# Retention, then a Mish feed-forward, on one core: block 0's second product by sub-block products, block 5's first product likewise, and output stores regrouped

## The chip, the cores and the metric

The kernel runs on one core of one Trainium2 chip. The metric is the time of one execution on the device in microseconds (us). Engines are called TensorE (PE, with PEld for its weight loads), VectorE (DVE), ScalarE (ACT), GpSimd (POOL) and SyncE (SP), which issues nearly all DMAs.

## The reference

`q`, `k`, `v` are 4 x 8 x 768 x 64 (batch, head, position, feature). A linear recurrence with a decay per head gives y, and y (3072 tokens by 512) goes through a feed-forward of width 2048:

```
for t in range(S):
    state = gamma * state + outer(k[t], v[t])
    y[t] = scale * (q[t] @ state)
x = y.transpose(0, 2, 1, 3).reshape(3072, 512)
h = x @ w_in                       # 512 x 2048
g = h * tanh(softplus(h))          # Mish
out = g @ w_out                    # 2048 x 512, float32
```

## The kernel before

**Tiling.** The sequence is cut into 24 chunks of 128 positions, and the chunks into eleven blocks: block 0 has four chunks (512 tokens), blocks 1 to 10 have two (256 tokens). For each chunk, q and k are scaled to fp16 and transposed; scores k·q are masked; "outer" products of k and v update the state; "present" (masked scores times v) and "past" (state times q) make y, which is copied to `xt` as the input of the feed-forward.

**Weights.** w_in and w_out come as four slices of 512 rows or columns each (`FPS` = 4 groups of 128), loaded in fp32 (`load_w`) and cast to fp16 (`cast_win`, `cast_wout`).

**First product** (`g1`): h = w_in · xt, in PSUM banks of 128x512, each followed by a Mish on ScalarE. Block 0 takes 16 banks (u = 0 to 15) with matmuls of 512 columns; blocks 1 to 5 take 8 with matmuls of 256 columns. Blocks 6 to 10 (`blk >= MIX`, `mixed_in`) compute two of the four w_in slices by seven sub-products instead of eight (a Strassen-like scheme): sums of weight quarters (`in_sums`, made once in blocks 4 and 5, kept in `wsum`), sums of xt quarters (`x_sums`, per block), 56 matmuls of 128 columns for these slices and 32 of 256 columns for the two other slices; partial results are kept in `hsum` tiles.

**Second product.** Block 0 computes g · w_out plainly: 16 groups by 4 token tiles, 64 matmuls of 512 columns into four banks (L649), with the attention work of block 1 placed between them by a table `plan`. Blocks 1 to 10 (`seven`) use seven sub-products over the whole width, with sums of w_out quarters (`weight_sums`, tiles `tmat`, t1 to t4) and sums of g (`sums_a`, `sums_b`, `sums_c`, tiles `gsum`, s1 to s4); ScalarE takes snapshots (`snap`), VectorE adds and writes the output tile `osb`.

**Order.** The schedule is written by hand: each engine runs its instructions in the order of the source, and waits on semaphores. `turn_two` transposes q and k of chunks 4 and 5 on TensorE into one PSUM tile `t_ps` and copies them out in four pieces; from chunk 6 on, GpSimd casts (`casts_qk`, `casts_v`) and SP transposes by DMA (`turn_by_dma`). `cast_behind` casts the coming chunks inside `seven`, behind a small copy (`summed`) that makes GpSimd wait until VectorE has made certain sums; `second_of` does the same for blocks 6 and later. Stores are queued in a list with a due slice, and `store_due` issues them from the loop over u of the following block; so SP issues, in one order, loads, DMA transposes and stores, each of which waits for what it needs with all later ones behind it. `get_ready(blk + 1)` makes outer products and scores of the next block, in slice u = 5 of blocks 1 to 3's first product; blocks 3 and later prepare the block after the next in `retain`.

Of the kernel before, what the change touches and what calls it, by code (L numbers as in the profile page):

```python
# [16 lines left out]
def kernel(  # L17
# [9 lines left out]
    nc = tc.nc  # L27
# [172 lines left out]
    def cast_win(s, by_tile=False):  # L200
        src = wtmps.pop(("in", s))
        wins[s] = []
        for j in range(2):
# [6 lines left out]
                nc.vector.tensor_copy(t, src[:, :, at0:at0 + TB // 2])  # L210
            wins[s].append(t)

    def cast_wout(s, on_act=False):
        src = wtmps.pop(("out", s))
        t = cpool.tile([P, FPS, d_model], FP16, name=f"wout{s}")
        if on_act:
            for f in range(0, FPS, 2):
                nc.scalar.copy(t[:, f:f + 2], src[:, f:f + 2])
        else:
            nc.vector.tensor_copy(t, src)  # L220
        wouts[s] = t

    def store_due(now):
        while stores and stores[0][0] <= now:
# [403 lines left out]
    def g1(blk, u):  # L628
        nt = BLOCKS[blk] * C
        per = TB // nt  # L630
        h_ps = g1_bank(blk, u)
        for j in range(per):
            s, f = divmod(u * per + j, FPS)
            for bp in range(NBP):
                nc.tensor.matmul(  # L635
                    h_ps[:, j], wins[s][f // 2][:, bp, f % 2 * P:(f % 2 + 1) * P], xts[blk][:, bp, :nt],
                    start=(bp == 0), stop=(bp == NBP - 1))
# [9 lines left out]
    def g2_mm(o_ps, blk, t, fb, cols=slice(None)):  # L647
        s, f = divmod(fb, FPS)
        nc.tensor.matmul(  # L649
            o_ps, gts[blk, fb][:, t * P:(t + 1) * P], wouts[s][:, f, cols],  # L650
            start=(fb == 0), stop=(fb == NFB - 1))
# [7 lines left out]
    def g2_out(o_ps, t, due):  # L659
        osb = op.tile(list(o_ps.shape), FP32, name="osb", tag="osb")  # L660
        if t == 0:
            nc.scalar.copy(osb, o_ps)
        else:
            nc.vector.tensor_copy(osb, o_ps)
        stores.append((due, out_rows(0, t), osb))

    def weight_sums(half):
        n, hf = NFB // 2, d_model // 2
        if half == 0:
            tmats.extend(  # L670
                wstage.tile([P, 2, n, hf], FP16, name="tmat", tag="wt", bufs=4)
                for _ in range(2))
            gsums.extend(
                wstage.tile([P, 4, n, P], FP16, name="gsum", tag="wt", bufs=4)
                for _ in range(2))
        f = slice(half * FPS, (half + 1) * FPS)
        t1, t2 = tmats[0][:, 0, f], tmats[0][:, 1, f]
        t3, t4 = tmats[1][:, 0, f], tmats[1][:, 1, f]
        b11, b12 = wouts[half][:, :, :hf], wouts[half][:, :, hf:]
        b21, b22 = wouts[half + 2][:, :, :hf], wouts[half + 2][:, :, hf:]  # L680
        sub = ALU.subtract
        return [
            lambda: nc.vector.tensor_tensor(t1, b12, b11, op=sub),
            lambda: nc.vector.tensor_tensor(t2, b22, t1, op=sub),
            lambda: nc.vector.tensor_tensor(t3, b22, b12, op=sub),
            lambda: nc.vector.tensor_tensor(t4, b21, t2, op=sub),
        ]
# [20 lines left out]
        nc.vector.tensor_tensor(s4, a12, s2, op=ALU.subtract)  # L708

    def in_sums(j):  # L710
        t = cpool.tile([P, 4, 2, TB // 2], FP16, name=f"wsum_{j}")
        wsums.append(t)
# [104 lines left out]
    def seven(blk, masks, hooks, last):  # L817
        n, hf = NFB // 2, d_model // 2
        px = pxps.tile([P, hf], FP32, name="o_ps", tag="px")
        pb = mmps.tile([P, hf], FP32, name="o_ps", tag="mm")  # L820
        osb = [op.tile([P, d_model], FP32, name="osb", tag="osb") for _ in range(2)]

        def a(i, j):
            return lambda f: gts[blk, j * n + f][:, i * P:(i + 1) * P]
# [136 lines left out]
    def first_block():  # L961
# [74 lines left out]
        def cast_qk():  # L1036
            for a in range(2):
                cast_pair(2, "q", a, qs_two)
            for a in range(2):
                cast_pair(2, "k", a)  # L1040
            for a in range(2):
                cast_pair(2, "v", a, vs_two)

        def turn_two():
# [5 lines left out]
            for a in range(2):  # L1050
                i = slice(a * (HP // 2), (a + 1) * (HP // 2))
                for j, nm in enumerate("qk"):
                    taken(pairs[2, nm + "t"][:, i], t_ps[:, j, i], False)

        def sum_weights(half, n):
            if not weight_left:
# [1 line left out]
            for _ in range(n):  # L1058
                weight_left.pop(0)()

        plan = {
            9: [(cast_wout, 0)],
            12: [(cast_wout, 1)],
            16: [(cast_wout, 2), (load_more,), (cast_qk,)],
            17: [(sum_weights, 0, 3)],
            23: [(cast_wout, 3, True)],
            25: [(turn_two,)],
            26: [(pair_scores, 2, 0)],
            27: [(pair_scores, 2, 1)],
            28: [(sum_weights, 0, 1), (turn_both, CPB + 2)],  # L1070
            29: [(outer_two,)],
            30: [(present_two,), (sum_weights, 1, 1)],
            31: [(y_two,)],
        }
        o_tiles = [None] * CPB
        for u in range(2 * NFB):
            if u < 2:
                if u == 0:
                    open_in(2)
            elif u < NFB:  # L1080
                g1(0, u)
            elif u < 2 * NFB - 2:
                w = u - NFB
                if w == 0:
                    for t in range(CPB):
                        pool, tag = (pxps, "px") if t == 0 else (mmps, "mm")
                        o_tiles[t] = pool.tile([P, d_model], FP32, name="o_ps", tag=tag)
                for t in range(CPB):
                    if t == CPB - 1 and w == 1:
                        g2_mm(o_tiles[t], 0, t, 0)  # L1090
                    if t < CPB - 1 or w > 0:
                        g2_mm(o_tiles[t], 0, t, w)
            else:
                for t in range(CPB // 2) if u % 2 == 0 else range(CPB // 2, CPB):
                    for w in range(NFB - 2, NFB):
                        g2_mm(o_tiles[t], 0, t, w)
                    g2_out(o_tiles[t], t, 0)
            for fn, *args in plan.get(u + 1, ()):
                fn(*args)

    def u_banks():
        t = atps.tile([P, 2, TB], FP32, name="u_ps", tag="at")
# [50 lines left out]
    def next_one(g):  # L1153
        load_to(g + 3)
# [21 lines left out]
    def cast_behind(blk, i):  # L1176
        g = first[blk] + (6 if blk == 1 else 8)
        if ncast[0] < min(g, NCK):
            nc.gpsimd.tensor_copy(summed, gsums[blk % 2][:, i, NFB // 2 - 1, P - 1:])  # L1179
            if blk == 1:  # L1180
# [2 lines left out]
                for n in range(g - 2, g):  # L1183
                    casts_v(n)
                ncast[0] = g
            elif blk + 1 >= MIX:
                cast_to(g - 2)
                casts_qk(g - 2)
                ncast[0] = g
            else:  # L1190
                cast_to(min(g, nload[0]))

    def tight(blk):

# [1 line left out]

    def plan_of(blk):
        a = first[blk] + 4
        plan = {u: [] for u in (0, 1, 5)}
        if tight(blk):  # L1200
            plan[5] = [(get_ready, blk + 1)]
# [10 lines left out]
    for blk in range(1, len(BLOCKS)):  # L1212
        last = blk + 1 == len(BLOCKS)
        plan = plan_of(blk)
        if blk >= MIX:
# [14 lines left out]
        if not last:  # L1230
            later = blk + 2 if ONE <= blk < len(BLOCKS) - 2 else None
            hooks = [[(retain, blk + 1, later)],
                     [(next_one, first[blk] + 6)] if blk + 1 >= MIX else
                     [(next_two, first[blk] + 6, tight(blk))] if blk >= ONE else
                     [(turn_load, first[blk] + 4)] if blk == 1 else
                     [(next_chunk, first[blk] + 5), (turn_load, first[blk] + 6)],
                     [(finish, blk + 1)] if later is None else []]
# [34 lines left out]
```

## Time and profile before

| What | Value |
|---|---|
| Time, median of 3 runs | 196.81 us (196.01 to 197.21) |
| The profiled execution: its own time, its span | 196.27 us, 194.5 us |
| Granted TensorE clock | 0.998 |
| TensorE's share of the chain that ended last | 93% |
| Block 0, first product / second product with what lies between | 19.5 to 31.6 / 31.6 to 48.9 us |
| Blocks 1, 2, 3 begin at | 48.86, 63.68, 78.52 us |
| Blocks 4, 5, 6, 7 begin at | 93.75, 108.20, 122.64, 136.85 us |
| Last store issued | 192.0 us |

The profile is one execution, seen from the span's start. Busy time is what the records of an engine cover; TensorE's matmuls are pipelined, so one matmul's own duration (273 ns for 256 columns) is longer than the distance to the next (109 ns), and sums are made with distances. "Idle before" names what an engine waited for before an instruction. The chain that ended last is followed back from the end; where TensorE is in it without a gap, a shorter engine elsewhere wins nothing. A block begins with the first matmul of its first product.

### The profile page before, as it was taken

The numbers are of one execution on the slowest core, as the hardware profiler recorded it, in microseconds if no ns is written. First come the engines' busy times: TensorE is split into PE (matmuls) and PEld (weight loads), VectorE is DVE, ScalarE is ACT, GpSimd is POOL, SyncE is SP. The second block draws the span as 40 slices with busy tenths as digits, with TensorE's granted clock in tenths as the row PEclk, the third lists the DMA queues.
The fourth block names the chain that finished last, engine by engine and source line by source line (L and its number), as shares of the span: only waits on it lengthen the run. The fifth ranks groups of instructions, "written<-read, shape, count | busy, mean of one in ns | idle before, by whom it ended". The sixth has DMA issues, their size and how long they took to land.

```text
span 194.5 us, 6886 instructions
## 1 busy us (share of the span) xinstructions
PE 189.6 (97%) x2996; PEld 154.0 (79%) x2996; DVE 128.7 (66%) x248; ACT 99.5 (51%) x183; POOL 73.3 (38%) x96
## 2 busy tenths in 40 slices
PE   7998999999999999999999999999999999999994
PEld 7756444454888888888888888998998998988983
DVE  0796535889767378467884864965885885876462
ACT  3375764243553552554364364584574663763750
POOL 5262000549508746562826605525625700000000
PEclk9999999999999999999999999999999999999999
DMA  5999999999999999999999999889996250300202
GB/s 172 304 309 349 368 386 366 293 302 202 202 260 248 157 233 225 214 175 216 261 207 227 278 192 287 103 225 245 77 223 123 50 150 5 111 0 20 95 27 81
DMA packets 84285, 38.75 MB, mean 199 GB/s; under 512 B 57760, under 2 KB 78880, under 8 KB 84256
## 3 DMA queue, kind: packets, MB, share of 16 engines
q1 hardware_dynamic: 84112, 38.28, 84.7%
q8 instruction: 23, 0.38, 0.9%
q10 hardware_dynamic: 144, 0.05, 0.1%
q14 instruction: 6, 0.05, 0.1%
HBM read 27.31 MB, written 6.29 MB: 173 GB/s over the span
## 4 chain that ended last, share of the span: by engine, by line
PE 93%; DMA 3%; ACT 1%; DVE 1%; issue 1%; SPq 0%
PE o_ps L838 32%; PE h_ps L635 24%; PE h_ps L765 9%; PE h_ps L745 8%; PE o_ps L649 7%; PE y_ps L551 3%; DMA qfirst<-in_q_dram 3%; PE u_ps L479 1%; PE at L472 1%; PE t_ps L247 1%; PE y_ps L373 1%; PE h_ps L620 1%; PE at L443 1%; PE at L327 1%; DVE qk L259 1%
## 5 line engine op out<-in xcount | busy, mean ns | idle before, releaser
L635 PE MATMUL h_ps<-xt,win 128*128 128x256 f16 (+1 forms) x376 | 48.5, 289 | 0.0
L635 PEld LDWEIGHTS <-win 128*128 128x128 f16 x376 | 36.5, 98 | 10.4 <-issue 0.2
L643 ACT ACTIVATE g<-h_ps 128x512 f16<-128x512 f32 x54 | 32.2, 597 | 23.7 <-PE h_ps L635 23.7
L838 PEld LDWEIGHTS <-gsum 128*128 128x128 f16 x320 | 30.3, 98 | 3.8
L838 PE MATMUL o_ps<-tmat,gsum 128*128 128x256 f16 x240 | 29.8, 273 | 0.0
L838 PEld LDWEIGHTS <-g 128*128 128x128 f16 x248 | 23.4, 98 | 2.7
L853 DVE TENSOR_TENSOR osb<-o_ps,snap 128x256 f32<-128x256 f32 (+1 forms) x33 | 13.8, 418 | 14.0 <-PE o_ps L838 8.9
L844 ACT COPY snap<-o_ps 128x256 f32<-128x256 f32 (+1 forms) x33 | 12.2, 370 | 20.7 <-PE o_ps L838 20.7
L414 POOL TENSOR_TENSOR qk<-qf,qvs 128x512 f16<-128x512 f32 x18 | 19.2, 1065 | 4.8 <-DMA qf<-in_q_dram 4.7
L765 PE MATMUL h_ps<-xt,win 128*128 128x256 f16 x160 | 20.7, 273 | 0.0
L424 POOL TENSOR_TENSOR v<-vf,qvs 128x512 f16<-128x512 f32 x18 | 19.7, 1101 | 1.2 <-DMA vf<-in_v_dram 1.0
L417 POOL TENSOR_TENSOR qk<-kf,qvs 128x512 f16<-128x512 f32 x18 | 19.1, 1060 | 2.7 <-DMA kf<-in_k_dram 2.6
L838 PE MATMUL o_ps<-wout,g 128*128 128x256 f16 x160 | 19.1, 273 | 0.0
L1179 POOL COPY summed<-gsum 128x1 f16<-128x1 f16 x7 | 3.0, 432 | 37.2 <-DVE gsum L704 29.8
L765 PEld LDWEIGHTS <-win 128*128 128x128 f16 x160 | 14.8, 98 | 1.4
L756 ACT ACTIVATE g<-h_ps 128x512 f16<-128x512 f32 x25 | 14.2, 588 | 2.4 <-PE h_ps L765 2.4
L600 ACT CAST xt<-y_ps 128x512 f16<-128x512 f32 x15 | 10.2, 734 | 10.2 <-PE y_ps L551 10.2
L649 PE MATMUL o_ps<-wout,g 128*128 128x512 f16 x64 | 15.0, 380 | 0.0
L780 DVE TENSOR_TENSOR hsum<-h_ps,hsum 128x512 f32<-128x512 f32 x15 | 10.4, 692 | 6.1 <-PE h_ps L745 4.4
L775 ACT COPY hsum<-h_ps 128x512 f32<-128x512 f32 x15 | 8.8, 585 | 10.5 <-PE h_ps L745 10.5
L699 DVE TENSOR_TENSOR gsum<-g 128x512 f16<-128x512 f16 x20 | 9.2, 459 | 5.2 <-ACT g L643 3.1
L507 DVE TENSOR_TENSOR mid<-u_ps,sth 128x256 f16<-128x256 f32 x15 | 6.3, 422 | 8.5 <-PE u_ps L479 8.2
(99 smaller groups left out, 277.7 us busy)
## 6 DMA issues: line engine op xcount, KB each, us to landing
kf<-in_k_dram SPq DMA_DIRECT2D x24, 256.0 KB, 5.3
vf<-in_v_dram SPq DMA_DIRECT2D x24, 256.0 KB, 5.5
out_dram<-osb SPq DMA_DIRECT2D x22, 256.0 KB, 3.5
qf<-in_q_dram SPq DMA_DIRECT2D x20, 256.0 KB, 4.3
wi<-in_moe_w_in_dram SPq DMA_DIRECT2D x6, 512.0 KB, 8.7
wt<-in_moe_w_out_dram SPq DMA_DIRECT2D x3, 1024.0 KB, 10.3
qfirst<-in_q_dram SPq DMA_DIRECT2D x2, 512.0 KB, 4.6
wi<-in_moe_w_in_dram SPq DMA_DIRECT2D x1, 1024.0 KB, 10.0
```

Source lines behind the costliest of these rows:

```text
L414: nc.gpsimd.tensor_tensor(in_place(q16.rearrange("p (w x) d -> p w x d", x=2)), by_head(qf), scale_by_head(qs_two[:, heads]), op=ALU.mult)
L417: nc.gpsimd.tensor_tensor(k16.rearrange("p (y w) d -> p w y d", y=2), kf.rearrange("p (w y) d -> p w y d", y=2), boosts.rearrange("p (w y) ...
L424: nc.gpsimd.tensor_tensor(cast[g][2], loaded.pop(g)[2], vs[g % 2].unsqueeze(2).broadcast_to((P, H, D)), op=ALU.mult)
L635: nc.tensor.matmul(h_ps[:, j], wins[s][f // 2][:, bp, f % 2 * P:(f % 2 + 1) * P], xts[blk][:, bp, :nt], start=(bp == 0), stop=(bp == NBP - 1))
L643: nc.scalar.activation(gt, h_ps, AF.Mish, scale=inv_boost3)
L649: nc.tensor.matmul(o_ps, gts[blk, fb][:, t * P:(t + 1) * P], wouts[s][:, f, cols], start=(fb == 0), stop=(fb == NFB - 1))
L745: nc.tensor.matmul(o_ps[:, f], w(f // 2, k)[:, f % 2 * P:(f % 2 + 1) * P], x[:, k], start=begin and f == 0 and k == 0, stop=k == 1, skip_g ...
L756: nc.scalar.activation(to, src, AF.Mish, scale=inv_boost3)
L765: nc.tensor.matmul(h_ps[:, f], wins[w][h // 2][:, k, h % 2 * P:(h % 2 + 1) * P], xts[blk][:, k, :2 * C], start=k == 0, stop=k == NBP - 1)
L838: nc.tensor.matmul(o_ps[:, cols], x(f), w(f)[:, cols], start=first and z == 0, stop=z == n - 1, skip_group_check=True)
L844: nc.scalar.copy(x, o_ps[:, cols])
L853: nc.vector.tensor_tensor(dst, o_ps[:, cols], plus, op=ALU.add)
```

## The change

- Block 0's second product: w_out slices 0 and 2 by seven sub-products (token halves by column halves), slices 1 and 3 plainly, all with 256 columns: 15 groups of 8 matmuls. The sums of g (`first_sums`) lie in the `wsum` tiles, before these are used for weights. Intermediate results (m1, m5, u2, u3, u35) are kept in `hsum` tiles by ScalarE (`kept_sum` without `plus`), VectorE or GpSimd.
- Its order, casts of w_out and attention work included, is written out in `first_out`. `turn_two` copies q on ScalarE and k on VectorE; the casts of v of chunks 4 and 5 come behind t4 on GpSimd.
- Block 0's first product from u = 5 on: two matmuls of 256 columns for one of 512.
- w_out slice 2 is loaded and cast in two halves.
- `MIX` = 5: block 5's first product is `mixed_in` too; `in_sums` move to blocks 2 and 3. A new `BACK` = 6 keeps the casts and DMA transposes where they were switched before; block 4's `cast_behind` casts q and k of both chunks ahead of both v.
- Stores: not issued in the loop over u any more. Those of blocks 0, 1 and 2 are issued in block 3's `seven`, between the DMA transposes and loads for chunks 14 to 17, block 3's at the start of block 4. Output tiles of blocks 1 to 3 lie in `hsum` buffers.
- Block 1 prepares block 2 in slice 6 rather than 5.

```
-    ONE, MIX = 3, 6
+    ONE, MIX, BACK = 3, 5, 6
...
-            if s < NSL - 1:
+            if s == NSL - 2:
+                for f in range(0, FPS, FPS // 2):
+                    at = s * FPS + f
+                    nc.sync.dma_start(t[:, f:f + FPS // 2], wout_ap[:, at:at + FPS // 2])
+            elif s < NSL - 2:
...
             for bp in range(NBP):
-                nc.tensor.matmul(
-                    h_ps[:, j], wins[s][f // 2][:, bp, f % 2 * P:(f % 2 + 1) * P], xts[blk][:, bp, :nt],
-                    start=(bp == 0), stop=(bp == NBP - 1))
+                wide = 2 * C if u >= 5 else nt
+                for at in range(0, nt, wide):
+                    cols = slice(at, at + wide)
+                    nc.tensor.matmul(
+                        h_ps[:, j, cols], wins[s][f // 2][:, bp, f % 2 * P:(f % 2 + 1) * P],
+                        xts[blk][:, bp, cols], start=(bp == 0 and at == 0), stop=(bp == NBP - 1),
+                        skip_group_check=blk == 0)
...
+    def first_sums():
...
+            lambda: nc.vector.tensor_tensor(s3, lo[:, :, :n], lo[:, :, n:], op=sub),
+            lambda: nc.vector.tensor_tensor(s1, lo[:, :, n:], hi[:, :, n:], op=add),
+            lambda: nc.vector.tensor_tensor(s2, s1, lo[:, :, :n], op=sub),
+            lambda: nc.vector.tensor_tensor(s4, hi[:, :, :n], s2, op=sub),
...
+    def first_out(load_more, cast_qk, cast_v, turn_two, sums, weight):
...
+        mm((0, 0), a(0, 0), b(0, 0))
+        m1 = kept_sum(banks[0, 0])
+        mm((0, 1), s(1), t(1))
+        m5 = kept_sum(banks[0, 1])
+        load_more()
+        cast_qk()
+        plain(1, 1, 1)
+        plain(0, 0, 1)
+        weight(0, 2)
+        mm((0, 0), a(0, 1), b(1, 0))
+        mm((0, 1), s(4), b(1, 1))
+        mm((1, 0), s(2), t(2))
+        u2 = kept_sum(banks[1, 0], m1)
+        weight(0, 1)
+        cast_v()
+        plain(0, 1, 1)
+        turn_two()
+        cast_wout(3, True)
+        mm((1, 0), s(3), t(3))
+        u3 = kept_sum(banks[1, 0], m1)
+        u35 = op.tile([P, 2, hf], FP32, name="hsum", tag="hsum", bufs=6)
+        nc.gpsimd.tensor_tensor(u35, u3, m5, op=ALU.add)
+        pair_scores(2, 0)
+        pair_scores(2, 1)
+        turn_both(CPB + 2)
+        mm((1, 0), a(1, 1), t(4))
+        plain(1, 0, 1)
+        plain(0, 1, 3, range(2))
+        outer_two()
+        plain(0, 0, 3, range(2))
+        plain(1, 0, 3, range(2))
+        present_two()
+        plain(0, 1, 3, range(2, FPS))
+        done(0, 1, u2)
+        plain(0, 0, 3, range(2, FPS))
+        done(0, 0)
+        y_two()
+        weight(1, 0)
+        plain(1, 0, 3, range(2, FPS))
+        done(1, 0, m1)
+        plain(1, 1, 3)
+        done(1, 1, u35)
+        for n in range(CPB):
+            stores.append((0, out_rows(0, n), osb[n]))
...
-                    taken(pairs[2, nm + "t"][:, i], t_ps[:, j, i], False)
+                    taken(pairs[2, nm + "t"][:, i], t_ps[:, j, i], nm == "q")
...
+            if u == 2 * FPS + FPS - 1:
+                sums, make = first_sums()
+                make[0]()
+                make[1]()
+                cast_wout(0)
+                sum_weights(0, 1)
+                make[2]()
+                cast_wout(1)
+                make[3]()
+                cast_wout(2)
...
-    def next_two(g, soon):
-        load_to(g + 3)
-        turn_next(g)
-        if soon:
-            turn_next(g + 1)
-        load_to(g + 4)
-        if not soon:
-            turn_next(g + 1)
+    def next_two(g):
+        if g == first[ONE] + 6:
+            for n in range(2):
+                store(2)
+                turn_next(g + n)
+            for n in (3, 4):
+                store(2)
+                load_to(g + n)
+        else:
+            for n in range(2):
+                turn_next(g + n)
+                load_to(g + n + 3)
...
         if blk >= MIX:
-            second_of(blk - 1)
+            store_due(NFB)
             mixed_in(blk, last)
-        elif blk > ONE:
-            weight_left.extend(in_sums(blk - ONE - 1))
+        elif blk in (2, 3):
+            weight_left.extend(in_sums(blk - 2))
+        elif blk == MIX - 1:
+            store(2)
         for u in range(NFB // 2 if blk < MIX else 0):
-            store_due(u)
             g1(blk, u)
```

More of the change, by code (lines that the diff above doesn't have):

```diff
@@ L211, in cast_win, with wout_tile @@
             wins[s].append(t)
+    def wout_tile(s):
+        if s not in wouts:
+            wouts[s] = cpool.tile([P, FPS, d_model], FP16, name=f"wout{s}")
+        return wouts[s]
     def cast_wout(s, on_act=False):
         src = wtmps.pop(("out", s))
-        t = cpool.tile([P, FPS, d_model], FP16, name=f"wout{s}")
-        if on_act:
+        t = wout_tile(s)
+        if s >= NSL - 2:
             for f in range(0, FPS, 2):
-                nc.scalar.copy(t[:, f:f + 2], src[:, f:f + 2])
+                (nc.scalar.copy if on_act else nc.vector.tensor_copy)(t[:, f:f + 2], src[:, f:f + 2])
         else:
             nc.vector.tensor_copy(t, src)
-        wouts[s] = t
     def store_due(now):
@@ L645, in g1 @@
             gts[blk, u * per + j] = gt[:, j]
[L647 to L651, printed above, removed]
     def out_rows(blk, t):
@@ L657, in out_rows @@
         return out[row0:row0 + P]
[L659 to L662, printed above, removed]
-        else:
-            nc.vector.tensor_copy(osb, o_ps)
-        stores.append((due, out_rows(0, t), osb))
+    def first_sums():
+        s = [win_sum_tile(j).rearrange("p a b c -> p (a b) c") for j in range(2)]
+        s1, s2, s3, s4 = (s[i // 2][:, i % 2 * FPS:(i % 2 + 1) * FPS] for i in range(4))
+        lo, hi = gtiles[0, 0][:, :FPS], gtiles[0, 1][:, :FPS]
+        n = TB // 2
+        add, sub = ALU.add, ALU.subtract
+        return (s1, s2, s3, s4), [
+            lambda: nc.vector.tensor_tensor(s3, lo[:, :, :n], lo[:, :, n:], op=sub),
+            lambda: nc.vector.tensor_tensor(s1, lo[:, :, n:], hi[:, :, n:], op=add),
+            lambda: nc.vector.tensor_tensor(s2, s1, lo[:, :, :n], op=sub),
+            lambda: nc.vector.tensor_tensor(s4, hi[:, :, :n], s2, op=sub),
+        ]
@@ L678, in weight_sums @@
         t3, t4 = tmats[1][:, 0, f], tmats[1][:, 1, f]
[L679 to L680 removed]
+        (b11, b12), (b21, b22) = [
+            (w[:, :, :hf], w[:, :, hf:]) for w in (wout_tile(half), wout_tile(half + 2))]
         sub = ALU.subtract
@@ L820, in seven @@
         pb = mmps.tile([P, hf], FP32, name="o_ps", tag="mm")
-        osb = [op.tile([P, d_model], FP32, name="osb", tag="osb") for _ in range(2)]
+        osb = [
+            op.tile([P, d_model], FP32, name="osb", tag="osb") if blk > ONE else
+            op.tile([P, d_model], FP32, name="osb", tag="hsum", bufs=6) for _ in range(2)]
         def a(i, j):
@@ L1059, in sum_weights @@
                 weight_left.pop(0)()
[L1061 to L1080, printed above, removed]
-                g1(0, u)
[L1082 to L1099, printed above, removed]
+        for u in range(NFB):
+            if u == 0:
+                open_in(2)
+            elif u > 1:
+                g1(0, u)
+            if u == 2 * FPS + FPS - 1:
[8 more added lines that the diff above has]
+                cast_wout(2)
+        first_out(load_more, cast_qk, cast_v, turn_two, sums, sum_weights)
     def u_banks():
@@ L1142, in next_chunk, with store @@
         load_to(g + 3)
-    def next_two(g, soon):
-        load_to(g + 3)
-        turn_next(g)
-        if soon:
-            turn_next(g + 1)
-        load_to(g + 4)
-        if not soon:
-            turn_next(g + 1)
+    def store(n):
+        for _ in range(n):
+            _, dst, osb = stores.pop(0)
+            nc.sync.dma_start(dst, osb)
+    def next_two(g):
[6 more added lines that the diff above has]
+                load_to(g + n)
+        else:
+            for n in range(2):
+                turn_next(g + n)
+                load_to(g + n + 3)
     def next_one(g):
@@ L1190, in cast_behind @@
             else:
-                cast_to(min(g, nload[0]))
+                both = range(ncast[0], min(g, nload[0]))
+                for n in both:
+                    casts_qk(n)
+                for n in both:
+                    casts_v(n)
+                ncast[0] = both.stop
     def tight(blk):
@@ L1198, in plan_of @@
         a = first[blk] + 4
-        plan = {u: [] for u in (0, 1, 5)}
+        ready_at = 6 if blk == 1 else 5
+        plan = {u: [] for u in (0, 1, ready_at)}
         if tight(blk):
-            plan[5] = [(get_ready, blk + 1)]
+            plan[ready_at] = [(get_ready, blk + 1)]
         elif blk < MIX:
```

52 lines of the change are left out of this document (47 added, 5 removed).

## The prediction

> **What bounds the kernel now.** I read the page first: TensorE is busy 97% of the span at full granted clock, and only the first slice and the last are thinner.
>
> ```profile
> PE 189.6 (97%) x2996; PEld 154.0 (79%) x2996; DVE 128.7 (66%) x248; ACT 99.5 (51%) x183; POOL 73.3 (38%) x96
> PE   7998999999999999999999999999999999999994
> PEclk9999999999999999999999999999999999999999
> DMA  5999999999999999999999999889996250300202
> ```
>
> So a microsecond is won by taking matmul columns away, and lost where TensorE starts to wait; other engines count only where they make it wait. Next the chain of waits in order of time (start, duration, what), for block 0's two products, for block 4's end, blocks 5 and 6:
>
> ```profile
> 19.50 12.09 PE h_ps L635 x56
> 31.59 7.77 PE o_ps L649 x36
> 39.36 0.89 PE t_ps L247 x16
> 40.25 0.86 PE o_ps L649 x4
> 41.11 0.40 PE at L327 x16
> 41.52 0.97 PE o_ps L649 x4
> ...
> 108.20 6.99 PE h_ps L635 x64
> ...
> 122.64 0.45 PE h_ps L745 x8
> 123.09 0.87 PE h_ps L765 x8
> 123.96 0.45 PE h_ps L745 x8
> ```
>
> The prices: a 512-column matmul 7.77/36 = 0.216 us, a 256-column one 6.99/64 = 0.109, a 128-column one 0.45/8 = 0.056, a group of 16 transposes 0.89, 16 score matmuls 0.35 (their row's 0.40 holds a 0.05 wait). Four 512-column matmuls take 0.86 after the transposes but 0.97 after the 64-row score matmuls: a return from 64-row tiles costs 0.11. Last, VectorE's and ScalarE's timeline and groups around block 0:
>
> ```profile
> 36.01 1.53 DVE L683 TENSOR_TENSOR tmat<-wout 128x1024 f16<-128x1024 f16 x1
> 40.29 1.42 DVE L253 COPY qkt<-t_ps 128x512 f16<-128x512 f16 x4 [0.70 <-PE t_ps L247]
> 44.03 1.40 DVE L686 TENSOR_TENSOR tmat<-wout,tmat 128x1024 f16<-128x1024 f16 x1
> ```
>
> ```profile
> L251 ACT COPY qkt<-t_ps 128x512 f16<-128x512 f16 x4 | 2.3, 583 | 2.5 <-PE t_ps L247 2.5
> L253 DVE COPY qkt<-t_ps 128x512 f16<-128x512 f16 x4 | 1.4, 418 | 0.7 <-PE t_ps L247 0.7
> ```
>
> The four copies after the transposes run back to back on VectorE and TensorE covers them with four 512-column matmuls. The first row is a 0.68 us operation stretched to 1.53 while GpSimd works.
>
> **Block 0's W_out product, columns.** Removed: the L649 pieces of the chain, 7.77, 0.86, 0.97, 1.83 and three more of 0.97 (the last four stand further on in that view): 14.34 for 64 matmuls. Added: 15 groups of 8 matmuls of 256 columns, 120 x 0.109 = 13.10, and three returns from 64-row tiles in the open (after the outer products, the present part and y), 0.33; a fourth falls into a wait below. From slice u=5 on, 44 matmuls of 512 columns in the first product become 88 of 256: 9.61 for 9.50, +0.11. Sum -0.80.
>
> **The same product, waits.** The changed kernel's instruction order shows a chain that before lacks. After the 16 transposes ScalarE copies a half of q, VectorE's copy of a half of k waits for it, ScalarE's second q half waits for that, the second k half for that, and VectorE's hsum u3 stands behind; TensorE's second scores wait for the last copy and the product with t4 for u3. From the transposes' end T: 0.58 + 0.42 + 0.58 + 0.42 (the rows above) + 0.69 (L780, the same 128x512 sum) = 2.69, with some 0.04 for each of four to five hand-overs (TensorE's end at 31.59, ScalarE's start at 31.62) 2.85. TensorE has s3·t3 (0.87) and two score groups (0.70) for it: 1.57. It waits 1.28. Without any hand-over cost it would be 1.1; with a sum still running on VectorE when the first k half is due, 1.6. I take 1.28.
>
> The Trainium skill's page "PSUM — Partial Sum Buffer" (Specifications) says that ScalarE and VectorE can read PSUM side by side where the banks differ, and q and k lie in two banks here; by it the four copies would take 1.2 us, not 2.0, and the wait would nearly vanish. No row of before has such a pair, and the listed semaphores forbid it.
>
> Everything else of block 0 is supply, which I walked by hand. VectorE ends its last w_in cast at 28.0; then s3 (0.68), s1 (from 28.8, when the twelfth activation is done), wout0 cast (1.23, landed 29.37) to 30.7, t1 to 31.4 (due 32.6), s2, wout1 cast (landed 32.09) to 33.3 (due 33.45), s4, wout2's two halves to 34.7 and 35.5 (due 35.2 and 35.6), t2 to 36.2, or 37.0 beside GpSimd (due 36.9). Margins are 0.1 to 1.2 and a late landing shows at once: 0 to 0.3. On ScalarE two snapshots, two copies and W_out slice 3's casts, which now stand behind the q copies (free at T + 1.65 = 41.2, landing 41.3), fit into its idle 5.38, 2.35 and 2.63 us; the casts have 1.6 us until plain(0,1,3). On GpSimd the v casts wait for t4 and u35 (1.1) ends about 43.8, when chunk 6's q landed before too. The next block's xt and banks have 0.5 us to spare. Block 0: -0.80 + 1.28 = +0.48, from +0.2 to +1.1.
>
> **Block 5's first product.** 64 matmuls (6.99) become what blocks 6 to 10 run: 0.45 + 0.87 + 0.45 + 0.87 + 1.34 + 0.87 + 0.45 + 0.87 + 0.52 = 6.69. That is -0.30. Its x_sums (four of 0.29) and hsums come onto VectorE; block 6 shows that they fit. The hsum buffers now hold osb of blocks 1 to 3 until stored; SP issues those stores before T16 (108.37 in before), and the sums are due from about 111: 0.
>
> **The moved rest.** in_sums (2.1 us) go from blocks 4 and 5 to 2 and 3, where VectorE idles 4.30 and 3.94 us before a mid: 0. get_ready of block 2 one slice later: same matmuls, 0. The stores: SP passes four of block 0, two each of blocks 1 and 2 behind the loads of chunks 8 to 15, so those loads and transposes go earlier; no row has TensorE waiting for a DMA, so nothing is gained, and they are paid in block 3, where T14 and T15 (chunks 14, 15) wait for GpSimd's casts and stores stand between. T17 is due at 119.5 in block 5 and was issued at 114.07 with 4.2 to landing, 118.3. Before, 14 entries from T14 to T17 took 16 us, 1.14 each; now 20 take 22.8, but T14 can follow its cast (93.4) rather than 97.99, into an empty queue: landing near 96, T17 near 119, due 120. Hidden by 1 us: 0, up to +2.
>
> **Sum.** The profiled run took 196.27 (span 194.5, 1.77 around it), 0.54 under the median 196.81. 196.27 + 0.48 - 0.30 = 196.45, say 196.5. Its own range, from the ends of the terms: 196.0 to 197.4.
>
> **Rivals.** A, the copy chain is covered (semaphores met earlier than I count, or the copies overlap): -0.80 - 0.30 gives 195.2. For it: ScalarE and VectorE are both idle there. Against: the waits are in the program. Chance 0.15.
>
> B, slower: GpSimd holds up block 5's x_sums. Block 4's tail now has casts of two chunks (six of 1.04 us from about 104 on) beside them; before, in blocks 6 to 10, GpSimd waits for x_sums. A row like L683's lost 0.8 us per operation to such company. Four x_sums would lose up to 3.2; h22's sum has 0.65 to spare in block 6 (mask done 125.88, two sums of 0.69, due 127.94). Three held up cost 1.75: 198.2. It decides once mask_two ends over 3.9 us after block 5's start. Against: GpSimd is done at 110 to 111, so the second pair likely goes free. Chance 0.15.
>
> C, slower too: the queue takes 1.25 per entry and T17 lands near 121, later if GpSimd's casts slip: 197.5 to 198.5. Chance 0.11.
>
> D, narrow matmuls are paced by their weight loads. Were each of block 5's 56 matmuls of 128 columns held to the 98 ns of its LDWEIGHTS row, they would cost 56 x (0.098 - 0.056) = 2.35 more: 198.8. Against: eight in 0.45, in each of blocks 6 to 10, so that loads overlap. Chance 0.02. The Trainium skill's page "TensorE: Matmul & The Clock Gate" (Back-to-back issue gap) speaks for D: it gives some 81 ns sustained for 128 columns, by which, as an estimate, block 5 would lose 1.4 us rather than win 0.30. The trace's 56 ns differs from it, and the trace decides.
>
> **How the numbers follow.** The forecast has 0.55, some mishap I don't see 0.02. 1% is 2 us, about what a measurement of this kernel can tell from no change. The forecast, A and half of B and C lie within it, less what scatter takes: 0.79. Slower by over 1% takes the larger halves of B and C, D and the unseen: 0.16. A full success is worth 1.1, half a per cent; faster by over 1% needs A and the runs' spread of 1.2 us on top: 0.05. The range goes from A less a little scatter, 195.0, to B, 198.2.
>
> **What would show it.** Right: the 256-column groups of block 0 at 0.87 for 8; TensorE waiting 1.1 to 1.6 us between 39 and 43 with the scores and the t4 product behind VectorE's qkt copy and hsum; block 1 starting near 49.3 (48.86 before); block 5's first product at 6.7; no wait of TensorE for a DMA. Wrong: copies side by side and block 1 at 48.2; a gap in block 5 behind mask or hsum; scores of block 7 waiting for a transposing DMA.

## The result, and the profile after

| | Before | After |
|---|---|---|
| Time, median of 18 runs each | 196.37 us | 197.61 us |
| Ratio, 95% interval | | 1.0052 (1.0039 to 1.0065) |
| The profiled execution: its own time, its span | 196.27, 194.5 us | 197.54, 195.8 us |
| Block 0, first product / W_out product with attention work | 13.84 / 17.32 us | 13.96 / 17.74 us |
| Blocks 1, 2, 3, 4 | 14.77, 14.84, 15.24, 14.44 us | 14.77, 14.84, 15.23, 14.45 us |
| Block 5 | 14.45 us | 15.09 us |
| Blocks 6 to 10 | 14.21, 14.04, 14.05, 13.77, 13.08 us | 14.21, 14.04, 14.04, 13.77, 13.09 us |

A length here goes from the start of a stage's first matmul to the start of the next stage's, block 10's to the end of its last matmul; block 0's first product is counted from its first 16 matmuls on, which stand at 17.6 us. One of the changed kernel's 18 runs took 383.03 us; the ratio leaves it out, and no profile shows what happened in it. The kernel became slower by half a per cent: 1.2 us in the medians, 1.27 us between the two spans. Two stages hold 1.18 of it: block 0 with 0.54 (0.12 + 0.42) and block 5 with 0.64; some 0.1 lies behind the last matmul, and every other block kept its length.

The page of the changed kernel first (busy time by engine, then the span in 40 slices of 4.9 us):

```profile
PE 189.0 (97%) x3120; PEld 164.1 (84%) x3120; DVE 133.1 (68%) x263; ACT 102.9 (53%) x191; POOL 73.4 (37%) x98
PE   7998999979999999999999998999999999999993
...
DMA  5999999999991999999999999999986260200202
GB/s 174 303 311 352 366 388 360 300 314 186 226 229 26 156 234 193 186 140 222 237 251 308 279 157 248 276 147 292 183 199 137 51 157 3 111 0 20 94 27 80
```

TensorE has two new dents, the ninth slice (39 to 44 us) and the twenty-fifth (117 to 122 us): that is where to look. The DMA row has a new hole too: in the thirteenth slice (59 to 64 us) the engines moved 26 GB/s, where before they were 9 or more tenths busy.

What TensorE waited for between 31 and 125 us, with total, times and longest:

```profile
PE at L335 <- DVE qkt L261: 0.9, 2, 0.7
PE at L480 <- DMA qkt<-qk: 0.6, 1, 0.6
PE o_ps L703 <- DVE hsum L688: 0.2, 1, 0.2
```

The first and third lie in block 0, the second in block 5. The chain of waits (start, duration, what) shows the first place step by step:

```profile
38.73 0.91 PE t_ps L255 x16
39.63 0.02 issue
39.66 0.59 ACT qkt L259
40.25 0.02 issue
40.27 0.44 DVE qkt L261
40.71 0.02 issue
40.73 0.59 ACT qkt L259
41.33 0.02 issue
41.35 0.04 DVE qkt L261
41.39 0.30 issue
41.69 0.69 DVE hsum L688
42.38 0.04 issue
42.42 2.34 PE o_ps L703 x20
```

ScalarE, VectorE, ScalarE, VectorE, one copy after the other, then the sum: 2.79 us from the end of the transposes to the product with t4. By the prediction's prices TensorE's own work in that stretch fills 1.57 of them.

The chain in block 5, the beginning of its first product and what follows it:

```profile
108.72 0.45 PE h_ps L854 x8
109.16 0.87 PE h_ps L874 x8
...
114.89 0.53 PE h_ps L854 x8
115.42 0.03 SPq L437
...
115.48 5.06 DMA qkt<-qk
120.54 0.04 issue
120.58 0.38 PE at L480 x24
```

Eight matmuls of 128 columns take 0.45 and eight of 256 take 0.87, and the first product ends at 115.42 after 6.70 us. There the chain leaves TensorE, which goes on with its second product meanwhile: it follows the transposing DMA of chunk 17 (T17): issued at 115.48, landed at 120.54, and the scores start at once behind it. VectorE's timeline shows a second wait, in brackets, a little earlier:

```profile
113.36 1.38 DVE L889 TENSOR_TENSOR hsum<-h_ps,hsum 128x512 f32<-128x512 f32 x2 [0.77 <-DMA out_dram<-osb]
```

The sum needs an `hsum` buffer that still held an output tile of block 3. The store that frees it landed at 113.24. Mish, and with it the first 16 matmuls of the second product, came late: these took 2.11 us instead of 1.91.

### The profile page after: what moved, and what is told of

Same layout as the page of the kernel before. It is cut to its first block, busy times and chain, and to the rows that moved or that the text cites. A ratio compares the mean times of both kernels' runs of the same rounds, so it can differ in the third digit from the quotient of the medians.

```text
span 195.8 us, 7173 instructions
## 1 busy us (share of the span) xinstructions
PE 189.0 (97%) x3120; PEld 164.1 (84%) x3120; DVE 133.1 (68%) x263; ACT 102.9 (53%) x191; POOL 73.4 (37%) x98
## 4 chain that ended last, share of the span: by engine, by line
PE 92%; DMA 3%; ACT 2%; issue 1%; DVE 1%; POOL 0%; POOLq 0%; SPq 0%
PE o_ps L949 30%; PE h_ps L646 21%; PE h_ps L874 11%; PE h_ps L854 10%; PE o_ps L703 7%; PE at L451 4%; PE y_ps L559 3%; DMA qkt<-qk 3%; PE t_ps L255 2%; PE at L480 1%; PE u_ps L487 1%; PE y_ps L381 1%; PE h_ps L628 1%; ACT qkt L259 1%; PE at L335 1%
## 5 line engine op out<-in xcount | busy, mean ns | idle before, releaser
L646 PE MATMUL h_ps<-xt,win 128*128 128x256 f16 (+1 forms) x356 | 41.5, 276 | 0.0
L646 PEld LDWEIGHTS <-win 128*128 128x128 f16 x356 | 34.6, 98 | 5.4
L655 ACT ACTIVATE g<-h_ps 128x512 f16<-128x512 f32 x46 | 27.5, 597 | 19.8 <-PE h_ps L646 19.8
L874 PE MATMUL h_ps<-xt,win 128*128 128x256 f16 x192 | 24.9, 273 | 0.0
L874 PEld LDWEIGHTS <-win 128*128 128x128 f16 x192 | 17.8, 98 | 1.6
L432 POOL TENSOR_TENSOR v<-vf,qvs 128x512 f16<-128x512 f32 x18 | 18.7, 1054 | 0.8 <-DMA vf<-in_v_dram 0.7
L865 ACT ACTIVATE g<-h_ps 128x512 f16<-128x512 f32 x30 | 17.1, 589 | 2.9 <-PE h_ps L874 2.9
L884 ACT COPY hsum<-h_ps 128x512 f32<-128x512 f32 x18 | 10.5, 586 | 12.7 <-PE h_ps L854 12.7
L889 DVE TENSOR_TENSOR hsum<-h_ps,hsum 128x512 f32<-128x512 f32 x18 | 12.5, 692 | 6.9 <-PE h_ps L854 4.4
L809 DVE TENSOR_TENSOR gsum<-g 128x512 f16<-128x512 f16 x20 | 8.6, 431 | 8.3 <-ACT g L655 6.0
L854 PE MATMUL h_ps<-xt,wsum 128*128 128x128 f16 x192 | 13.7, 219 | 0.0
L865 ACT ACTIVATE g<-hsum 128x512 f16<-128x512 f32 x18 | 11.4, 631 | 1.8 <-DVE hsum L889 1.8
```

The lines of the kernel that those rows point to most:

```text
L432: nc.gpsimd.tensor_tensor(cast[g][2], loaded.pop(g)[2], vs[g % 2].unsqueeze(2).broadcast_to((P, H, D)), op=ALU.mult)
L646: nc.tensor.matmul(h_ps[:, j, cols], wins[s][f // 2][:, bp, f % 2 * P:(f % 2 + 1) * P], xts[blk][:, bp, cols], start=(bp == 0 and at == 0) ...
L854: nc.tensor.matmul(o_ps[:, f], w(f // 2, k)[:, f % 2 * P:(f % 2 + 1) * P], x[:, k], start=begin and f == 0 and k == 0, stop=k == 1, skip_g ...
L865: nc.scalar.activation(to, src, AF.Mish, scale=inv_boost3)
L874: nc.tensor.matmul(h_ps[:, f], wins[w][h // 2][:, k, h % 2 * P:(h % 2 + 1) * P], xts[blk][:, k, :2 * C], start=k == 0, stop=k == NBP - 1)
L889: nc.vector.tensor_tensor(m, x, y, op=ALU.add)
```

## The experiments

Nine kernels, each the changed kernel with one to three edits. "W_out" is block 0's second product with the attention work in it, "waits" are TensorE's between 31 and 125 us in the profiled execution, as the list of waits has them. Spans and stages are those of one profiled execution, the ratio that of all runs.

| Kernel | W_out | Block 5 | Waits of TensorE | Span | Ratio to before (95%) |
|---|---|---|---|---|---|
| the change | 17.74 | 15.09 | copies 0.9, hsum 0.2, T17 0.6 | 195.8 | 1.0052 (1.0039 to 1.0065) |
| qk_apart | 16.90 | 15.26 | hsum 0.2, hsum in block 5 1.0 | 194.9 | 1.0010 (0.9994 to 1.0027) |
| copies_dve | 17.14 | 14.48 | copies 0.2, hsum 0.2 | 194.6 | 1.0006 (0.9984 to 1.0028) |
| stores_back | 17.94 | 14.51 | copies 0.9, hsum 0.2 | 195.7 | 1.0038 (1.0012 to 1.0064) |
| t17_first | 18.17 | 14.31 | copies 0.9, w_out cast 0.3, hsum 0.2 | 195.4 | 1.0051 (1.0025 to 1.0078) |
| after_plain5 | 17.72 | 15.56 | copies 0.9, hsum 0.2, T17 1.0 | 196.5 | 1.0076 (1.0048 to 1.0104) |
| qk_t17 | 16.78 | 14.17 | hsum 0.2 | 194.1 | 0.9969 (0.9949 to 0.9988) |
| both | 16.66 | 14.96 | hsum 0.2, hsum in block 5 0.4 | 194.5 | 0.9984 (0.9966 to 1.0001) |
| apart_plain5 | 16.57 | 14.44 | hsum 0.2 | 194.2 | 0.9989 (0.9974 to 1.0004) |
| best | 16.80 | 14.15 | hsum 0.2 | 193.9 | 0.9962 (0.9947 to 0.9977) |

The theory: block 0 loses by the chain of copies, and block 5 by what the moved stores push back. The rivals: the copies cost little and the rest of block 0 (supply, narrower matmuls) takes the time; block 5's own seven products, or GpSimd's casts beside its sums, cost more than they win.

### Block 0: is it the chain of copies?

**qk_apart** gives q and k a PSUM tile each:

```
-            t_ps = atps.tile([P, 2, HP, 2, C], FP16, name="t_ps", tag="at")
+            t_ps = [atps.tile([P, HP, 2, C], FP16, name="t_ps", tag="at") for _ in range(2)]
...
-                    taken(pairs[2, nm + "t"][:, i], t_ps[:, j, i], nm == "q")
+                    taken(pairs[2, nm + "t"][:, i], t_ps[j][:, i], nm == "q")
```

> The change with the transposed q and k of chunks 4 and 5 in two PSUM tiles, so that ScalarE's copies of q and VectorE's of k don't wait for each other. Theory (the chain of four copies is what TensorE waits for in block 0, 1.1 us in three pieces): the copies run side by side, the first scores start 1.2 us after the transposes' end and the other two pieces vanish, wait in all 0.4; block 1 starts near 48.7 for 49.43. The queue's wait in block 5 then grows by what TensorE comes earlier, so that the span falls by less, to 195.4 to 195.8. Rival (other work on VectorE holds the scores): block 1 starts at 49.4 as now.

**copies_dve** keeps the one tile and lets VectorE make all four copies, as the kernel before did:

```
-                    taken(pairs[2, nm + "t"][:, i], t_ps[:, j, i], nm == "q")
+                    taken(pairs[2, nm + "t"][:, i], t_ps[:, j, i], False)
```

> The change with all four copies of q and k on VectorE, in one PSUM tile, as before. Theory (the hand-overs between the engines cost, not the copies): done 1.42 us after the transposes' end for 2.1; the second scores wait 0.25 for 0.66 and the t4 product 0.35 for 0.18, the first none; block 1 starts near 48.9 for 49.43. Rival (TensorE lacks cover, whoever copies): the wait stays at 1.0 or more and block 1 starts at 49.3 or later.

Of qk_apart the timelines of ScalarE and then of VectorE:

```profile
39.37 1.07 ACT L259 COPY qkt<-t_ps 128x512 f16<-128x512 f16 x2 [0.21 <-PE t_ps L255]
```

```profile
39.81 0.76 DVE L261 COPY qkt<-t_ps 128x512 f16<-128x512 f16 x2 [0.41 <-PE t_ps L255]
40.69 0.69 DVE L688 TENSOR_TENSOR hsum<-o_ps,hsum 128x512 f32<-128x512 f32 x1
```

Both engines now wait for TensorE's transposes alone and copy at the same time: q from 39.37 to 40.44, k from 39.81 to 40.57, and the sum follows at 40.69, 1.00 earlier than in the change. The stage takes 16.90 and not 17.74. Four more kernels with two tiles (below) took 16.57 to 16.80, and four with the chain 17.72 to 18.17. With all copies on VectorE (1.42 for the four, no wait between them) it is 17.14.

The spread within each kind is one place: before the stage's 17th matmul TensorE waits from 0 to 0.45 for the cast of w_out's slice 1, which VectorE starts at 31.98 in the change and, held by the landing of the slice, at 32.41 in t17_first. With this wait taken off, the kernels with two tiles stand at 16.55 to 16.60, those with the chain at 17.71 to 17.74, and copies_dve at 17.01. So the chain cost 1.15 us against two tiles and 0.72 against copies on VectorE alone, and it came from the two engines' turns at one tile, not from a bank that can't serve them both: with q and k in separate tiles neither engine waited for the other. That agrees with the page "PSUM — Partial Sum Buffer" (Specifications) of the Trainium skill, by which both engines can read PSUM in parallel while their banks differ; in the change they lay in two banks and the semaphores still put them in a row.

### Block 5: is it the moved stores?

**stores_back** issues the stores from the loop over u again, and the loads and transposing DMAs of block 3 in the order that they had before the change:

```
         if g == first[ONE] + 6:
-            for n in range(2):
-                store(2)
-                turn_next(g + n)
-            for n in (3, 4):
-                store(2)
-                load_to(g + n)
+            load_to(g + 3)
+            turn_next(g)
+            turn_next(g + 1)
+            load_to(g + 4)
...
-        elif blk == MIX - 1:
-            store(2)
         for u in range(NFB // 2 if blk < MIX else 0):
+            store_due(u)
             g1(blk, u)
```

> The change with the stores of blocks 0 to 3 issued from the loops again, as before; all else as changed. Theory (the moved stores alone make the second transposing DMA for block 7 land at 120.5, 0.6 us after TensorE needs it, and hold a sum of block 5 back by 0.8): no TensorE wait for a DMA in block 5, VectorE's hsum waits for no store, block 5 takes 14.1 to 14.2 us for 15.09, span near 194.9 for 195.8. Rival (the transposing DMA is late because block 5's product is shorter and GpSimd's casts are ordered otherwise): the wait of 0.6 stays and the span is within 0.2 of 195.8.

No wait of TensorE for a DMA and no wait of VectorE for a store was left, and block 5 took 14.51 instead of 15.09. So the moved stores cost 0.58 there, or more. The span does not show it (195.7, where 194.9 was expected): in this profile TensorE begins the first product 0.22 later, the wait for w_out's slice 1 is 0.23, and block 4 takes 0.08 more, so that the ratio can't be told from the change's either. Block 5 is not the 14.1 to 14.2 expected; VectorE's timeline shows why, with the change's row for the first pair of x_sums behind it:

```profile
107.95 1.94 DVE L841 TENSOR_TENSOR xt<-xt 128x256 f16<-128x256 f16 x2
...
110.48 0.66 DVE L841 TENSOR_TENSOR xt<-xt 128x256 f16<-128x256 f16 x2
```

```profile
107.45 0.62 DVE L841 TENSOR_TENSOR xt<-xt 128x256 f16<-128x256 f16 x2
```

The first two x_sums take 0.62 in the change, where GpSimd idles, and here 1.94. With the loads of chunk 17 back in time, GpSimd casts chunks 16 and 17 from 105.16 to 112.35 almost without a pause, right over these sums. That is rival B of the prediction.

**t17_first** leaves the stores where the change has them, and puts block 4's two transposing DMAs ahead of its two loads:

```
             for n in range(2):
                 turn_next(g + n)
+            for n in range(2):
                 load_to(g + n + 3)
```

> The change with the stores left where it put them, but in block 4 both transposing DMAs (chunks 16, 17) stand ahead of both loads. Theory (the queue's order makes it late; GpSimd's cast for it ends at 113.0 but SyncE issues it at 115.5 behind a load): it is issued near 113 and lands near 118, the wait of 0.6 is gone, VectorE's 0.8 for a store stays; span near 195.1. Rival (GpSimd's late cast, 3.7 us behind a load, is what makes it late): it still lands after 120 and the span stays at 195.8.

The wait is gone: T17 was issued at 112.99 and landed at 117.16, and block 5 took 14.31, 0.78 less than in the change. VectorE's wait for a store, which was expected to stay, came to less than 0.15, since VectorE was later itself: its second pair of x_sums took 1.33 beside a cast. In the profiled execution block 0 gives 0.43 of the gain back, in the wait for w_out's slice 1 (the prediction has this cast done at 33.3 and due at 33.45). The timed ratio shows no gain at all; its ten runs go from 196.86 to 198.82 us, and what the other nine lost is not shown. The ratio alone would have said that the order of these DMAs is worth nothing; the stage says otherwise.

**after_plain5** takes the opposite side: block 5's first product plain again, the stores still moved (block 4's, behind T17 in both, wait until block 6 here).

```
-    ONE, MIX, BACK = 3, 5, 6
+    ONE, MIX, BACK = 3, 6, 6
...
-        elif blk == MIX - 1:
+        elif blk == ONE + 1:
             store(2)
```

> The change with block 5's first product plain, stores deferred as in the change. If the deferred stores alone make chunk 17's transposes late: TensorE waits for them 0.2 to 0.4 (the plain product asks for them 0.3 later), block 5 at 14.65 to 14.85; VectorE's wait for a store to free an hsum buffer is gone. Rival (the seven products are needed for the delay): block 5 at 14.45 and no wait for a DMA.

```profile
PE at L480 <- DMA qkt<-qk: 1.0, 1, 1.0
```

The wait for T17 is there without the seven products, and apart_plain5 (below), plain as well but with the stores back, has none; so it belongs to the stores. Its size was missed: 1.0, not 0.2 to 0.4. T17 took 5.85 us from issue (115.37) to landing, against 5.06 in the change; why the same transfer took longer was not tried. Nor is the size fixed otherwise: in copies_dve, whose stores are those of the change, T17 landed at 119.28, and the stretch of its scores took 0.87 where the change has 1.34 and best 0.60, a loss of 0.27 that the list of waits doesn't show.

Where did the queue lose its time? SyncE's timeline, first before, then of the change, from block 0's stores to T17:

```profile
95.14 0.44 SPq L162 DMA_DIRECT2D qf<-in_q_dram  x1
...
97.99 3.96 SPq L429 DMA_TRANSPOSE qkt<-qk  x2
102.00 0.57 SPq L162 DMA_DIRECT2D qf<-in_q_dram  x1
...
108.37 3.32 SPq L429 DMA_TRANSPOSE qkt<-qk  x1
...
114.07 2.23 SPq L429 DMA_TRANSPOSE qkt<-qk  x1
```

```profile
92.47 2.67 SPq L1238 DMA_DIRECT2D out_dram<-osb  x2
95.24 1.30 SPq L437 DMA_TRANSPOSE qkt<-qk  x1
96.63 1.03 SPq L1238 DMA_DIRECT2D out_dram<-osb  x2
97.76 1.46 SPq L437 DMA_TRANSPOSE qkt<-qk  x1
99.32 1.24 SPq L1238 DMA_DIRECT2D out_dram<-osb  x2
100.61 0.45 SPq L162 DMA_DIRECT2D qf<-in_q_dram  x1
...
102.84 2.14 SPq L1238 DMA_DIRECT2D out_dram<-osb  x2
105.03 0.46 SPq L162 DMA_DIRECT2D qf<-in_q_dram  x1
...
107.12 3.74 SPq L1238 DMA_DIRECT2D out_dram<-osb  x2
110.97 1.30 SPq L437 DMA_TRANSPOSE qkt<-qk  x1
...
115.48 2.68 SPq L437 DMA_TRANSPOSE qkt<-qk  x1
```

Ten stores where the kernel before had four in this stretch. The load of chunk 16 is issued at 100.61 (before: 95.14), that of chunk 17 at 105.03 (102.00), T16 at 110.97 (108.37), T17 at 115.48 (114.07). Chunk 16's load also changed places with T14 and T15; but ahead of chunk 17's load the same entries stand before and after, and six stores more. GpSimd waits 3.7 us for chunk 17's q:

```profile
110.92 1.04 POOL L422 TENSOR_TENSOR qk<-qf,qvs 128x512 f16<-128x512 f32 x1 [3.73 <-DMA qf<-in_q_dram]
```

SyncE takes 3.74 us over the two stores of block 3, whose last piece VectorE wrote by 94.73, so that their data were long there. SyncE's waits put 3.3 of this down to a VectorE operation (L524) that ended at 110.37, but that one writes no output, and in five more kernels with these stores the same entry takes 2.9 to 3.2 whatever VectorE ends then. That leaves the entries ahead of them as the likely reason; no view shows it directly. And the time that the stores gave back earlier bought nothing, as the same engine's waits between 54 and 63 us show:

```profile
SPq L437 <- POOL qk L425: 7.5, 1, 7.5
```

With the loads ahead of it issued, SyncE stood for 7.5 us at a transposing DMA until GpSimd had made the cast, and issued it at 62.01 (before: at 61.49, with four stores issued meanwhile). Between 50 and 87 us the DMA engines moved 6.41 MB instead of 8.05; six stores of 0.26 MB make 1.6. They were moved out of a stretch with room into one that had none.

### Do the repairs add up, and what else is in block 5?

**both** is stores_back and qk_apart in one.

> The change with q and k of turn_two in two PSUM tiles and the stores issued from the loops again. If the two repairs add up: W_out stage 16.9 (after 17.74), block 5 near 14.5 with no wait of TensorE for a DMA, span near 194.4, ratio to before 0.998 to 1.001. Rival: block 0 that ends 0.8 us earlier meets a later limit (supply of chunks by the queue), and the 0.8 comes back as waits in blocks 1 to 5; then the span stays near 195.

**best** adds to these an edit for GpSimd: `ONE, MIX, BACK = 3, 5, 5`, so that chunk 17's q and k are cast behind block 5's x_sums, as blocks 6 and later do it.

> As the last one, and the casts of chunks 16 and 17 split as from block 6 on (chunk 17's q and k behind block 5's x_sums). If GpSimd beside the x_sums was what was left in block 5: the first pair of x_sums takes 0.6, not 1.9, block 5 takes 14.15 to 14.2, span near 194.0, ratio 0.996 to 0.999. Rival: chunk 17's transposing DMA, issued later, is late again: block 5 at 14.5 or more, with TensorE waiting for qkt.

**apart_plain5** is both with block 5's first product plain (`MIX, BACK = 6, 6`): of the change's larger parts, only block 0 and the earlier `in_sums` are left.

> Two PSUM tiles for q and k, stores from the loops, and block 5's first product plain again, so that of the change's three parts only block 0's is left: W_out stage 16.9, block 5 14.45, span 194.2 (0.3 under before), ratio 0.997 to 1.000. If best takes 0.3 less than this one in block 5, the seven products are worth there what the forecast said (-0.30).

W_out took 16.57 to 16.80 in all three; what it won did not come back as waits in blocks 1 to 4. In **both** block 5 took 14.96, not the 14.5 expected and more than the 14.51 of stores_back: GpSimd's casts now run without a pause from 103.65 to 109.84, the x_sums beside them are stretched again, and TensorE waits 0.4 for an hsum. In **best** VectorE and GpSimd look like this:

```profile
108.13 0.48 DVE L841 TENSOR_TENSOR xt<-xt 128x256 f16<-128x256 f16 x2
...
110.94 0.69 DVE L889 TENSOR_TENSOR hsum<-h_ps,hsum 128x512 f32<-128x512 f32 x1
```

```profile
104.78 1.04 POOL L425 TENSOR_TENSOR qk<-kf,qvs 128x512 f16<-128x512 f32 x1
108.75 0.19 POOL L1259 COPY summed<-xt 128x1 f16<-128x1 f16 x1 [2.93 <-DVE xt L841]
108.89 1.04 POOL L422 TENSOR_TENSOR qk<-qf,qvs 128x512 f16<-128x512 f32 x1
```

GpSimd is made to wait 2.93 us for the last x_sum, the sums take their short time, and block 5 takes 14.15, 0.29 less than plain (14.44). The Trainium skill's page "SBUF — State Buffer" (SBUF: two separate sides) says that GpSimd and VectorE hold a shared port as a lock for a whole instruction, the other one blocking. The trace agrees in kind: of sums that take 0.29 alone, the first two in stores_back take 0.81 and 1.09 beside casts of 1.04.

best beats the kernel before by 0.4% (0.23 to 0.53) and the change by 0.9% (0.9962 / 1.0052).

**qk_t17** joins qk_apart and t17_first, to see what the wait for the stores of block 3 costs by itself.

> The change with two PSUM tiles for q and k and with block 4's transposing DMAs ahead of its loads; stores deferred as in the change. What is left against the best version is the wait of VectorE's hsum for the stores of block 3 (its output tiles lie in hsum buffers) and GpSimd's casts beside x_sums. If that wait is a cost of its own: TensorE waits for hsum or g, 0.7 to 1.0 us in all, block 5 at 14.9 to 15.2, W_out stage 16.7 to 16.9, span 194.6 to 194.9. Rival: the late transposing DMA was all that cost anything; block 5 at 14.2 to 14.3, span 194.0.

```profile
112.45 0.69 DVE L889 TENSOR_TENSOR hsum<-h_ps,hsum 128x512 f32<-128x512 f32 x1 [0.59 <-DMA out_dram<-osb]
```

VectorE still waits 0.59 for a store, but TensorE waits for nothing in block 5, which takes 14.17: the rival was right, and the moved stores cost next to nothing once T17 stands ahead of the loads. In qk_apart, with one transposing DMA and one load in another order, the same kind of wait came at the third sum, and TensorE lost 1.03. (It is 0.80 there, after 1.10 before the second sum; the view puts that down to TensorE, but the first of the two stores landed at 112.57, 0.12 before this sum began.) So this wait is a margin of some 0.6 us that the landing of two stores passes or not: it cost nothing in qk_t17, 0.2 in the change and 1.03 in qk_apart.

## Why the prediction was right or wrong

**No change was forecast, and the kernel became slower.** The forecast was no change that can be told (196.5, range 195.0 to 198.2); the time was 197.61, slower by 0.52%, with an interval (0.39% to 0.65%) that leaves no doubt of it. The prediction took 1% for about what a measurement can tell here; 18 runs of each told half of that. The time lies inside the range, but in part by luck: the range owes its upper end to rival B, which did not happen in the change. In spans, the sum said +0.18 and the trace has +1.27.

**Block 0 was right, term by term.** First product +0.11 forecast, +0.12 measured. W_out: columns and returns -0.91, wait +1.28, together +0.37; measured +0.42, and block 1 at 49.43 in the chain (49.3 forecast). By the distances between matmul starts, TensorE loses 0.33 before the first scores, 0.80 before the second and 0.25 before the t4 product, in all 1.38; the list of waits counts from the end of the matmul before and has 0.26, 0.66 and 0.18. Columns and returns are then -0.90, with 0.06 of waiting that before had at its scores. The steps of the copies (0.59, 0.44, 0.59 and the 0.69 sum) are those that the rows gave. Rival A fell.

**Block 5's product was right.** 6.70 us for its first product (6.69 forecast), and -0.29 for the block between apart_plain5 and best (-0.30 forecast). Rival D fell by the same rows: 8 matmuls of 128 columns in 0.45. (The 1.4 that is given beside D comes on top of the forecast; with the 0.30 won it would have been a loss of 1.1.)

**The failed step is the price of the moved stores**, "T14 can follow its cast (93.4) rather than 97.99, into an empty queue: landing near 96, T17 near 119, due 120. Hidden by 1 us: 0". The rate in it was good: 20 entries from T14's landing to T17's took 21.3 us, 1.07 each (1.14 counted). The start was not: T14 landed at 99.24, 3.24 behind the forecast. GpSimd's cast for it:

```profile
92.90 1.04 POOL L425 TENSOR_TENSOR qk<-kf,qvs 128x512 f16<-128x512 f32 x1
```

It ended at 93.94, 0.5 later than counted. SyncE issued T14 at 95.24, 1.3 behind the cast, because the first two moved stores stood ahead of it; these could not go before 92.47, since ahead of them stood the loads of chunks 14 and 15, behind transposing DMAs that SyncE finished issuing only at 87, in both kernels. And T14 took 4.0 us from issue to landing, where the step has 2.6; no transposing DMA whose landing the kernel before shows took under 3.08. The faster rate gave 1.5 of the 3.24 back, and T17 landed at 120.54. The step took it that entries freed early let later ones go early; but the early stretch stood empty, as SyncE's wait of 7.5 us for a cast shows, and the queue at T14 was not. Against block 5's 14.15 in best, the stretch around T17's scores is longer by 0.74 (1.34 from the first of them to the second product's last part, 0.60 in best), the slow 16 matmuls behind the late hsum by 0.20: together the 0.94 that turn 14.15 into 15.09.

**The second zero, the hsum buffers**, rested on "SP issues those stores before T16 (108.37 in before), and the sums are due from about 111". Issuing is not landing: block 3's stores were issued at 107.12 to 110.86 and landed at 113.24 and 113.89.

**The rivals.** C has the outcome, with T17 at 120.54 where it said near 121 and a time of 197.5 to 198.5, but not the way: it has the queue take 1.25 per entry, and the entries took 1.07 from a later start. It was given 0.11. B did not happen in the change, since chunk 17's late load kept GpSimd idle during the x_sums; it happened as soon as the load was in time, at a lower price than its 1.75: against best, block 5 is 0.36 longer in stores_back and 0.81 in both. Removing one delay uncovered the next.

What stays open: how T17's landing time depends on what moves beside it, and what holds SyncE at the first of block 3's stores.

## What to carry to other kernels

Moving a transfer later frees its slot only if something is ready to use it: find out first what paces the queue at the place that it leaves, and count the entries from a landing that the trace shows, not from when the data are ready. Where a late transfer is needed by a fixed time, its place in the order can matter more than the number of entries: T17 ahead of two loads made the moved stores all but free. A tile that two engines read in turns chains them by semaphores even where they can run side by side; two tiles made nothing else wait here and won 1.15 us in the stage. When a repair of one wait brings less than it should, look for an engine that now runs at a time when it used to be starved.

## What the runs showed of the hardware

VectorE's 128x256 sums of fp16, 0.28 to 0.29 us each alone, took 0.46 to 1.13 beside GpSimd's 1.04 us casts (stores_back, both); the change had hidden that by starving GpSimd. The transposing DMA of one chunk took 5.06 us from issue to landing in the change and 5.85 in after_plain5, at the same place in the order; before, T17 took 4.52 (114.07 to 118.59).
